# E and F loaded on 128 partitions, V and the first w_in piece in parts, a normalize one step earlier: a change to the opening of an attention and FFN kernel

## The chip, the cores and the metric

The kernel runs on one core of one Trainium2 chip. The metric is the device time of one execution in microseconds (us). The time before the change is a median of 484.24 us over three runs (483.96 to 484.36). All runs here are on one core. Some executions of a kernel can fall in a slower state (a lower granted clock, or a time over 1.5% above the fastest). None that was timed in rounds (several executions of each kernel of a call) was in it; of the single runs, whose state can't be told, only the profile is used. Times inside an execution are counted from the start of its span, as the profile counts them. PE is TensorE's matmul side, PEld its weight loads, DVE is VectorE, ACT is ScalarE, POOL is GpSimd and SP is SyncE.

## The reference

Linear attention of eight batches feeds a two-layer FFN. All inputs are float32.

```
k_proj = einsum('ks,bhsd->bhkd', E, k)      # E, F: 64 x 1024
v_proj = einsum('ks,bhsd->bhkd', F, v)      # q, k, v: 8 batches, 8 heads, 1024 tokens, 64 wide
attn   = softmax(q @ k_proj^T / sqrt(64)) @ v_proj
x      = attn, heads side by side           # 8192 x 512
h      = relu(x @ w_in)                     # w_in 512 x 2048
out    = (h * h) @ w_out                    # w_out 2048 x 512
```

## The kernel before

The kernel is one long run of matmuls: while the FFN of a batch runs, the attention of the next is slipped in between its matmuls. Only batch 0 has nothing to hide behind, so its attention is cut in half (half the tokens first). The loads of K, Q, V, w_in and w_out convert to bfloat16 on the way and go, in this order, through GpSimd's DMA queue. E and F go through SyncE's queue, as float32, on 64 partitions.

```python
    e_f32 = []
    for src in (E, F):
        t = relu_pool.tile([KP, S], F32, tag="h_relu", name="e_f32")     # 64 x 1024
        nc.sync.dma_start(t[:], src[:])
        e_f32.append(t)
    ...
    def load_heads(t, src, g):
        s = slice(4 * g, 4 * g + 4)
        nc.gpsimd.dma_start(t[:, s], rows(src, 0)[:, s])
    ...
    for g in range(2):
        load_heads(K_first, k, g)
    ident = const_pool.tile([P, P], BF16, name="ident")
    make_identity(nc, ident[:])
    load_q_half(0, slice(0, H))
    for g in range(2):
        load_heads(V_first, v, g)
    ...                                  # then w_in, the rest of Q, w_out
    def E_and_F():
        for t, src, copy in ((ET, e_f32[0], nc.vector.tensor_copy), (FT, e_f32[1], nc.scalar.copy)):
            e_bf = soft_pool.tile([KP, S], BF16, tag="expT", name="e_bf")
            copy(e_bf[:], src[:])
            ps = ffn_psum("ps_E", (P, NI, KP), BF16)
            view = e_bf[:].rearrange("k (p i) -> k i p", i=NI)
            for i in range(NI):
                nc.tensor.transpose(ps[:, i, :], view[:, i, :], ident[0:KP, 0:KP])
            copy(t[:], ps[:])
```

The stages of batch 0, in order. The fillers are matmuls whose result nobody uses; they keep PE occupied.

```python
            filler(2)
            self.project_k(0)
            filler(1)
            self.transpose_k(0)
            self.project_k(1)
            filler(2)
            self.transpose_k(1)
            filler(1)
            ...                          # transposes of Q, scores, exponentials
            self.project_v(0)
            self.copy_v(0)
            ...                          # sums, reciprocals
            self.half_values(0)
            self.half_normalize(0, 0, 0)
            self.project_v(1)
            self.copy_v(1)
            self.half_normalize(0, 0, 1)
```

The softmax here doesn't subtract the row's maximum and nothing guards it: scores larger than these inputs give would overflow.

## Time and profile before

| what | before | where it is read |
|---|---|---|
| median time | 484.24 us | the timed runs |
| span, PE busy | 482.0 us, 470.4 us | first lines of the page |
| E landed, F landed | 4.61, 5.89 us | the trace's DMA completion records |
| K's first half: the 16 DMA engines done | 7.51 to 8.25 us | same |
| first K projection starts | 8.61 us | timeline of PE |
| full clock from | 12.37 us | the trace's clock record |
| first FFN matmul | 20.01 us | timeline of PE |

The clock record gives the share of its clock that TensorE is granted. The matmuls of the K projections are 0.213 us apart ahead of the rise at 12.37 us and 0.109 after it.

The head of the page of the kernel before: PE is busy 470.4 of 482.0 us, so at most 11.6 us could be won without touching a matmul.

```profile
span 482.0 us, 8383 instructions
PE 470.4 (98%) x3614; PEld 293.1 (61%) x3614; DVE 313.2 (65%) x380; ACT 261.8 (54%) x414; POOL 33.2 (7%) x46
```

The timeline of PE from 4 to 24 us (start, duration, engine, source line, operation, output<-inputs, sizes, count; in brackets how long PE had been idle and what released it):

```profile
5.58 0.70 PE L141 MATMUL ps_E<-ident,e_bf 64*128 64x64 bf16 x8 [5.58 <-DVE e_bf L137]
7.01 0.70 PE L141 MATMUL ps_E<-ident,e_bf 64*128 64x64 bf16 x8 [0.73 <-ACT e_bf L137]
7.64 1.03 PE L360 MATMUL ps_fill<-ET 128*128 128x512 bf16 x2
8.61 1.92 PE L260 MATMUL ps_k<-K_sb,ET 128*64 128x256 bf16 x8
...
11.61 1.42 PE L260 MATMUL ps_k<-K_sb,ET 128*64 128x256 bf16 x8
...
20.01 0.81 PE L459 MATMUL ps_h<-xT,w_in 128*128 128x512 bf16 x3 [0.37 <-DVE xT L350]
```

PE transposes E, waits for F's cast, transposes F, runs two fillers and then the first K projection. The chain of work that ended last: its pieces in order of time, up to the first K projection (start, duration, what):

```profile
1.38 4.51 DMA e_f<-in_F_dram
...
5.91 1.05 ACT e_bf L137
...
7.01 0.70 PE ps_E L141 x8
7.71 0.96 PE ps_fill L360 x2
8.68 1.86 PE ps_k L260 x8
```

The chain starts with F's load and not with K's. But K is close behind: its last DMA engine finished at 8.25, less than 0.4 us before PE used it. This is the transfer view of E and F, then that of K's two halves, for the kernel before:

```profile
DMA to landing us min/median/max: 3.9/4.2/4.5
```

### The profile page before, as it was taken

Reading aid. Unit: us, or ns where it says so; the run is one execution under the profiler, and the core shown is the slowest. Engines: PE = TensorE matmul, PEld = TensorE weight load, DVE = VectorE, ACT = ScalarE, POOL = GpSimd, SP = SyncE. Lnnn points to the kernel's source line nnn. Section 1 sums busy time; section 2 is a strip of 40 time slices with the busy share of each in tenths; the row PEclk is TensorE's granted clock in tenths of the full one; section 3 lists DMA queues with packets and bytes.
Section 4 is the critical chain, followed back from the end, with each engine's and each line's share of the span. In section 5 each row is a group of like instructions: output and inputs, shape, how many; then the busy total and the mean of one; then the engine's idle time right before and its main releaser. Section 6 shows DMA issues by size and latency. Waiting matters only on the chain.

```text
span 482.0 us, 8383 instructions
## 1 busy us (share of the span) xinstructions
PE 470.4 (98%) x3614; PEld 293.1 (61%) x3614; DVE 313.2 (65%) x380; ACT 261.8 (54%) x414; POOL 33.2 (7%) x46
## 2 busy tenths in 40 slices
PE   4899999999999999999999999999999999999997
PEld 2544776475575746657475665747557474666656
DVE  1478855555958558493876748666594855948383
ACT  2488544758426664466635657176662756545351
POOL 6340020020020001000010000100000000000000
PEclk9999999999999999999999999999999999999999
DMA  9999989479989075931859147590712002020202
GB/s 162 204 204 207 170 184 203 124 128 227 172 124 238 6 176 89 192 80 64 145 87 229 13 121 131 90 196 1 173 3 81 20 1 88 1 88 0 88 0 88
DMA packets 72501, 55.46 MB, mean 115 GB/s; under 512 B 33936, under 2 KB 64656, under 8 KB 72464
## 3 DMA queue, kind: packets, MB, share of 16 engines
q0 software_dynamic: 30336, 29.36, 39.0%
q1 hardware_dynamic: 42128, 25.56, 21.2%
q8 instruction: 28, 0.46, 0.4%
q14 instruction: 9, 0.07, 0.0%
HBM read 59.24 MB, written 16.78 MB: 158 GB/s over the span
## 4 chain that ended last, share of the span: by engine, by line
PE 93%; DVE 3%; ACT 2%; DMA 1%; issue 0%; SPq 0%
PE ps_h L459 44%; PE ps_y L479 23%; PE ps_z L479 11%; PE ps_x L479 6%; PE ps_kv L178 3%; PE ps_att L219 2%; PE ps_att L204 2%; DVE hsq L518 1%; DMA e_f<-in_F_dram 1%; PE ps_k L260 1%; DVE s L473 1%; DVE xT L244 0%; ACT expT L313 0%; DVE xT L350 0%; ACT h_relu L510 0%; PE ps_fill L360 0%
## 5 line engine op out<-in xcount | busy, mean ns | idle before, releaser
L459 PE MATMUL ps_h<-xT,w_in 128*128 128x512 bf16 x1024 | 225.0, 379 | 0.4 <-DVE xT L350 0.4
L518 DVE TENSOR_TENSOR hsq<-h_relu 128x1024 bf16<-128x1024 f32 x123 | 150.0, 1223 | 76.7 <-ACT h_relu L510 76.1
L510 ACT ACTIVATE h_relu<-ps_h 128x512 f32<-128x512 f32 x256 | 149.8, 597 | 62.6 <-PE ps_h L459 62.4
L459 PEld LDWEIGHTS <-w_in 128*128 128x128 bf16 x1024 | 99.6, 98 | 117.9 <-issue 1.7
L479 PEld LDWEIGHTS <-s 128*128 128x128 bf16 x1024 | 98.5, 98 | 19.8 <-issue 8.7
L479 PEld LDWEIGHTS <-hsq 128*128 128x128 bf16 x768 | 73.8, 98 | 16.4 <-issue 2.9
L479 PE MATMUL ps_y<-T,s 128*128 128x256 bf16 x512 | 62.4, 273 | 0.0
L595 DVE TENSOR_TENSOR o_sb<-ps_z,p_b 128x512 f32<-128x512 f32 x16 | 11.1, 691 | 54.7 <-ACT p_b L591 21.1
L473 DVE TENSOR_TENSOR s<-hsq 128x1024 bf16<-128x1024 bf16 x64 | 43.5, 684 | 0.0
L591 ACT COPY o_sb<-ps_y 128x512 f32<-128x512 f32 x15 | 8.8, 586 | 54.2 <-PE ps_y L479 54.1
L211 ACT ACTIVATE expT<-ps_att 128x1024 bf16<-128x1024 f32 x28 | 27.2, 1025 | 14.0 <-PE ps_att L204 14.0
L244 DVE TENSOR_TENSOR xT<-ps_att,rs 128x1024 bf16<-128x1024 f32 x28 | 33.4, 1216 | 0.6 <-PE ps_att L219 0.6
L479 PE MATMUL ps_x<-w_out,hsq 128*128 128x256 bf16 x256 | 33.2, 273 | 0.0
L479 PE MATMUL ps_y<-w_out,hsq 128*128 128x256 bf16 x256 | 33.2, 273 | 0.0
L479 PE MATMUL ps_y<-T,hsq 128*128 128x256 bf16 x256 | 30.9, 272 | 0.0
L479 PE MATMUL ps_z<-T,s 128*128 128x256 bf16 x256 | 30.6, 273 | 0.0
L479 PE MATMUL ps_z<-w_out,s 128*128 128x256 bf16 x256 | 30.6, 273 | 0.0
L591 ACT COPY p_b<-ps_y 128x512 f32<-128x512 f32 (+1 forms) x17 | 9.4, 556 | 25.9 <-PE ps_y L479 25.8
L473 DVE TENSOR_TENSOR s<-s,hsq 128x1024 bf16<-128x1024 bf16 x32 | 21.9, 686 | 0.3
L473 DVE TENSOR_TENSOR s<-hsq,s 128x1024 bf16<-128x1024 bf16 x32 | 21.8, 684 | 0.0
L81 POOL DMA_DIRECT2D Q_sb<-in_q_dram x7 | 6.1, 877 | 226.1 <-DMA qT<-Q_sb 225.7
L591 ACT COPY p_a<-ps_y 128x512 f32<-128x512 f32 (+1 forms) x17 | 9.4, 561 | 21.8 <-PE ps_y L479 21.6
(74 smaller groups left out, 232.0 us busy)
## 6 DMA issues: line engine op xcount, KB each, us to landing
out_dram<-o_sb SPq DMA_DIRECT2D x30, 512.0 KB, 3.1
K_sb<-in_k_dram POOLq DMA_DIRECT2D x7, 1024.0 KB, 15.4
V_sb<-in_v_dram POOLq DMA_DIRECT2D x7, 1024.0 KB, 22.4
Q_sb<-in_q_dram POOLq DMA_DIRECT2D x7, 1024.0 KB, 9.8
w_in<-in_moe_w_in_dram POOLq DMA_DIRECT2D x8, 256.0 KB, 13.6
w_out<-in_moe_w_out_dram POOLq DMA_DIRECT2D x4, 512.0 KB, 13.3
K_sb<-in_k_dram POOLq DMA_DIRECT2D x2, 512.0 KB, 7.9
V_sb<-in_v_dram POOLq DMA_DIRECT2D x2, 512.0 KB, 12.7
```

The source lines that it names most:

```text
L178: nc.tensor.matmul(ps[0:KP, :], lhsT=ET[:, i, :], rhs=kv[:, :, i, :], start=f, stop=l)
L204: nc.tensor.matmul(ps[o, bank, :], lhsT=self.kT[r, 2 * pr + j, :], start=True, stop=True, rhs=self.qT[r, NT * (2 * pr + j):NT * (2 * pr + ...
L211: nc.scalar.activation(e[:], self.ps["s", pr][:], AF.Exp, scale=SCALE)
L219: nc.tensor.matmul(ps[32 * j:32 * j + 32, a, :], lhsT=weights(o, 4 * g + j), rhs=self.exp[2 * g + j // 2][o, bank, :], start=True, stop=Tr ...
L244: nc.vector.tensor_tensor(out=self.xT[:, 2 * g + e].rearrange("p a n t -> p a (n t)"), in0=self.ps["v", g, e][:], in1=self.rs[g][:], op=AL ...
L459: nc.tensor.matmul(ps[:], lhsT=w_in_blk(cb, fb), rhs=xT[:, cb, :, 2 * ch:2 * ch + 2], start=(cb == 0), stop=(cb == NCB - 1),)
L473: nc.vector.tensor_tensor(out=s[o][:, js], in0=x, in1=y, op=op)
L479: nc.tensor.matmul(ps[tb] if len(ps) == 2 else ps[0][:, tb], lhsT=lhs[:, j, tb * P:(tb + 1) * P], rhs=rhs[:, j], start=first and n == 0 an ...
L510: nc.scalar.activation(r[:, n], ps[:], AF.Relu)
L518: multiply = lambda: nc.vector.tensor_tensor(out=o, in0=r[:], in1=r[:], op=ALU.mult)
L591: nc.scalar.copy(to[:, t], ps)
L595: nc.vector.tensor_tensor(out=to[:, t], in0=ps, in1=more[:, t], op=ALU.add)
```

## The change

Its intent is to start the FFN sooner. E and F are loaded on 128 partitions (two half rows per row of E), so that the load is faster and the casts are on twice the partitions; the transposes become small matmuls that pick even or odd rows. V's second head group is loaded and projected in two parts, and all values of the first half come before the FFN. The first w_in piece is loaded in two parts. One relu goes to DVE, and in the later batches one normalize is issued one step earlier (behind step 25 instead of 26).

```diff
-        t = relu_pool.tile([KP, S], F32, tag="h_relu", name="e_f32")
-        nc.sync.dma_start(t[:], src[:])
+        t = relu_pool.tile([P, S // 2], F32, tag="h_relu", name="e_f32")
+        nc.sync.dma_start(t[:], src.rearrange("k (c s) -> (k c) s", c=2))
 ...
-    for g in range(2):
-        load_heads(V_first, v, g)
+    for s in (slice(0, 4), slice(4, 6), slice(6, 8)):
+        load_heads(V_first, v, s)
 ...
-            nc.gpsimd.dma_start(w_in_sb[j][:, g], w_in_view[:, g, :, j * fw:(j + 1) * fw])
+            for n in range(2) if (j, g) == (0, 0) else (slice(None),):
+                s = slice(n * fw // 2, (n + 1) * fw // 2) if n in (0, 1) else n
+                nc.gpsimd.dma_start(
+                    w_in_sb[j][:, g, :, s], w_in_view[:, g, :, j * fw:(j + 1) * fw][:, :, s])
 ...
+        pick = ident[:].rearrange("p (k c) -> p c k", c=2)
 ...
-            e_bf = soft_pool.tile([KP, S], BF16, tag="expT", name="e_bf")
+            e_bf = soft_pool.tile([P, S // 2], BF16, tag="expT", name="e_bf")
             copy(e_bf[:], src[:])
-            ps = ffn_psum("ps_E", (P, NI, KP), BF16)
-            view = e_bf[:].rearrange("k (p i) -> k i p", i=NI)
+            ps = ffn_psum("ps_E", (P, NI, KP))
+            view = e_bf[:].rearrange("r (p i) -> r i p", i=NI)
             for i in range(NI):
-                nc.tensor.transpose(ps[:, i, :], view[:, i, :], ident[0:KP, 0:KP])
+                for c, o in enumerate((LO, HI)):
+                    nc.tensor.matmul(ps[o, i, :], lhsT=view[:, i, :], rhs=pick[:, c, :], start=True, stop=True)
             copy(t[:], ps[:])
 ...
-            self.half_normalize(0, 0, 0)
-            self.project_v(1)
-            self.copy_v(1)
-            self.half_normalize(0, 0, 1)
+            for s in heads[1:]:
+                self.project_v(s)
+                self.copy_v(s)
+            self.half_values(1)
+            for g in range(2):
+                for e in range(2):
+                    self.half_normalize(0, g, e)
 ...
-        23: "sums 0, values 0 0, reciprocals 0", 26: "normalize 0 0",
+        23: "sums 0, values 0 0, reciprocals 0", 25: "normalize 0 0",
 ...
-                nc.scalar.activation(r[:, n], ps[:], AF.Relu)
+                if (b, ch, k, n) == (0, 0, 0, 1):
+                    nc.vector.tensor_scalar_max(r[:, n], ps[:], 0.0)
+                else:
+                    nc.scalar.activation(r[:, n], ps[:], AF.Relu)
```

Cut: the bookkeeping of the V parts, and the opening FFN steps, which no longer stop after three matmuls to wait for V's second group.

## The prediction

> **What bounds the kernel now.** The page's engine table gives PE (TensorE matmul) 470.4 us busy of a 482.0 us span; stretches of ten microseconds show PE at 10.00 of 10 almost everywhere after 40 us. PE idles 11.6 us: 5.6 at the start, about 3.5 at the end, about 2.5 between 6 and 37 us. Only the start can give anything.
>
> **What bounds the start.** The DMA stream, and behind it a chain of small steps. The timeline has the first K projection at 8.60 us, just after the first half of K landed (8.25 by the trace's DMA semaphores); later pieces land every 2.6 us per 512 KB: 10.85 (K), 13.50 (Q), 15.99, 18.54 (V), then 19.88 and 21.97 (first w_in piece; its last DMA engine lags 0.8). The first FFN matmul starts at 20.01; three run, PE waits for V's second group (projected 18.58 to 19.64, copied 19.88 to 20.29), then runs closed up from 21.10, but for 0.2 us at 24.1 while ScalarE empties the opening's four banks.
>
> **Step 1, E and F on 128 partitions.** They are issued first on 64 partitions and land at 4.61 and 5.89 us. Their 4096-byte packets take 0.16 us at first, then 0.33, and the first K packet moves only at 4.19, 2.95 us after its issue; loads issued later into an idle queue take about 1.6. The Trainium skill, "SBUF — State Buffer", section "Door 1: The DMA port swizzle", says that 64 partitions reach half of the ports; the doubled packet time agrees. On 128 partitions I expect 0.5 MB in about 1.3 us instead of some 3, so K, and the whole stream behind it, lands about 1 us earlier. The casts of E and F (0.89, 1.04 us) about halve. Added: 32 small matmuls for 16, and a float PSUM copy of ET (estimate 0.65 us, from 0.42 for 256 float columns, against 0.42); both fit before K's landing.
>
> **Step 2, V in parts.** One projection becomes two of half the columns (sum equal, or 0.3 us longer by weight loads), one copy of 0.41 us two of about 0.25. But all four normalizes (0.68 each) now queue on DVE behind both copies, and all values precede the FFN: its first matmul comes later against the chain, then runs without a break. Estimate: 0 to 0.3 us lost.
>
> **Step 3, w_in in two parts; relu on DVE.** The first part landing sooner matters little once the normalize is last. The relu on DVE should remove the 0.2 us gap. The moved later normalize lies where PE never waits: nothing.
>
> **Sum.** 1.1 us from DMA; minus 0.3, because more of K's projection runs at the cold clock (its matmuls are 0.213 us apart before 12.3 us, 0.109 after); minus 0.2 for V's order; plus 0.2 for the gap. Net 0.8 us, kept to the end because PE is saturated.
>
> **Prediction:** 483.4 us, range 482.6 to 484.3. Chances: faster by over 2% 0.01, within 2% 0.98, slower 0.01.
>
> **What would show it.** Right: E and F landed by about 4.5 us, first K packet near 3.3, K landed near 7.2, K projection near 7.4, FFN closed up from about 19.7, no gap after the opening, PE busy time within 1 us. Wrong for step 1: K still landing at 8.25, so descriptor making and not E and F held it. Wrong for step 2: the opening held by V's second copy or by DVE.
>
> **What would make it wrong.** The clock rising later (idle PE between fillers and K), a straggling DMA engine on w_in's second part, V's small matmuls bound by weight loads: then 484 or more. A stream that gains 1.5 us: 482.5.

## More of the kernel before

For later batches a table says behind which FFN step each piece of attention goes. The two entries that matter here:

```python
        23: "sums 0, values 0 0, reciprocals 0", 26: "normalize 0 0",
        28: "scores 2, scores 3, exponentials 2", 29: "exponentials 3",
```

```profile
L94 POOL DMA_DIRECT2D K_sb<-in_k_dram x2: 750/819/888, 1.2 to 2.1; - x2
DMA to landing us min/median/max: 7.0/7.9/8.7
```

K's first half was issued at 1.2 us and took 7.0 us, its second was issued at 2.1 and took 8.7.

## The result, and the profile after

The kernel after took a median of 484.84 us (six runs, 484.45 to 485.37), beside 484.3 us for the kernel before on the same chip (six runs, 483.92 to 484.5). The ratio is 1.0013, with a 95% interval from 1.0001 to 1.0026. A ratio here is the mean time of one kernel's fast runs over that of the other's from the same rounds, so it is not quite the ratio of the medians. The change was expected to save 0.8 us and cost 0.6, and the median lies above the range of 482.6 to 484.3.

One warning before the profiles are compared. The profiled execution of the kernel after took 485.37 us, the slowest of its six, and that of the kernel before took 483.81, below all six of its timed runs. The two traces therefore differ by 1.56 us, more than twice what the medians do. They show the mechanism; how much of it an average run pays must come from the timed runs.

The head of the page after: PE's busy time grew by 1.1 us and the span by 1.6.

```profile
span 483.6 us, 8454 instructions
PE 471.5 (98%) x3645; PEld 293.7 (61%) x3646; DVE 314.3 (65%) x382; ACT 260.9 (54%) x413; POOL 34.4 (7%) x48
```

The timeline of PE after, the same stretch:

```profile
4.35 2.13 PE L147 MATMUL ps_E<-ident,e_bf 128*64 128x64 bf16 x32 [4.35 <-POOL ident masks.py:199]
6.41 1.03 PE L364 MATMUL ps_fill<-ET 128*128 128x512 bf16 x2
9.78 1.86 PE L265 MATMUL ps_k<-K_sb,ET 128*64 128x256 bf16 x8 [2.33 <-DMA K_sb<-in_k_dram]
...
12.73 1.91 PE L265 MATMUL ps_k<-K_sb,ET 128*64 128x256 bf16 x8
...
22.52 1.67 PE L462 MATMUL ps_h<-xT,w_in 128*128 128x512 bf16 x7 [0.19 <-DVE xT L354]
```

E and F are transposed by 6.48 us instead of 7.71, as intended. The fillers end at about 7.44. Then PE waits 2.33 us for K, and the K projection starts 1.17 us later than before. The clock also rises later (16.04 us instead of 12.37), so the second projection takes 1.91 us where it took 1.42. PE's idle time is the likely reason. The clock record of r7 below changes in steps of 3.41 us; counted back in such steps from the two rises, PE was busy for 93% of the stretch from 8.96 to 12.37 before, and for 77% of that from 9.21 to 12.62 after. But the busy share alone does not decide it over all traces: in r5 the clock rose after a stretch with 83%, and in r1 it did not rise after one with 89%. The chain of work that ended last now begins with K:

```profile
1.25 8.49 DMA K_sb<-in_k_dram
...
9.78 1.88 PE ps_k L265 x8
```

The transfers of E and F, then of K, in the kernel after:

```profile
DMA to landing us min/median/max: 2.9/3.0/3.1
```

```profile
L93 POOL DMA_DIRECT2D K_sb<-in_k_dram x2: 747/816/886, 1.2 to 2.1; - x2
DMA to landing us min/median/max: 8.5/9.3/10.2
```

E and F land in 2.9 and 3.1 us instead of 3.9 and 4.5. K, issued at the same moment, takes 8.5 us instead of 7.0. The trace also records, for each load, when each of the 16 DMA engines was done with its share; this is where the loss becomes plain:

| load (us) | before: first, 14th, 15th, last engine | after: first, 14th, 15th, last engine |
|---|---|---|
| E | 4.00, 4.46, 4.53, 4.61 | 3.27, 3.54, 3.58, 3.65 |
| F | 5.33, 5.77, 5.82, 5.89 | 3.95, 4.19, 4.22, 4.26 |
| K, first half | 7.51, 8.04, 8.22, 8.25 | 6.68, 7.16, 8.72, 9.73 |
| K, second half | 10.27, 10.73, 10.74, 10.85 | 9.64, 10.05, 11.32, 12.32 |
| Q, first half | 12.93, 13.36, 13.36, 13.50 | 12.33, 12.69, 13.95, 14.96 |
| V, first group | 15.47, 15.89, 15.89, 15.99 | 14.85, 15.19, 16.47, 17.49 |

Fourteen engines of the kernel after finish K's first half by 7.16 us, very nearly the 7.2 that was predicted for the whole of it. Two finish at 8.72 and 9.73. The Trainium skill, "DMA: Bandwidth & Descriptors", section "Why a DMA increments its semaphore by 16 and not by 1", says that the engines of a transfer finish independently and that only the full 16 means that all data landed. The trace agrees: PE starts at 9.78, behind the last engine, with 14 of 16 shares in place for 2.6 us. GpSimd's queue shows no gap in its packets until 59.2 us, and a late engine stays late: the distance from first to last is 3.05 us for K's first half and then 2.68, 2.63, 2.64 us for the next three loads, and still 2.63 for the first w_in piece.

**Where the 1.6 us of the two traces lie.** I paired the FFN matmuls of the two kernels by number, and took the difference of their starts. The 41st FFN matmul starts at 30.63 before and at 32.68 after: +2.05 us. By the 1024th it is +1.60 (465.93 and 467.53). The +2.05 is the later K projection (+1.17) and a longer way from there to the fifth FFN matmul (12.72 us before, 13.60 after: +0.88). The 0.45 that comes back later falls mostly in five equal steps of 0.078 us, one in each of the later batches two to six; their place is the moved normalize. In the timeline of the kernel before, around 166 us, the scores of heads 2 and 3 use a PSUM bank (a piece of the memory that matmuls write to) that the normalize of line 244 still reads:

```profile
165.02 1.22 DVE L244 TENSOR_TENSOR xT<-ps_att,rs 128x1024 bf16<-128x1024 f32 x1
165.99 0.70 PE L204 MATMUL ps_att<-qT,kT 64*64 64x512 bf16 x8
166.29 0.11 PEld L204 LDWEIGHTS <-kT 64*64 64x64 bf16 x4 [0.18 <-DVE xT L244]
```

The same place after: the normalize started one step sooner and ended at 166.81, before the scores begin. There is one block of eight weight loads with no wait for DVE, and the scores take 0.63 us instead of 0.70.

```profile
165.58 1.23 DVE L249 TENSOR_TENSOR xT<-ps_att,rs 128x1024 bf16<-128x1024 f32 x1 [3.40 <-ACT rs L239]
```

```profile
167.98 0.14 PEld L209 LDWEIGHTS <-kT 64*64 64x64 bf16 x8 [0.21 <-issue]
167.98 0.63 PE L209 MATMUL ps_att<-qT,kT 64*64 64x512 bf16 x8
```

**The gap after the opening.** The relu on DVE was to close a gap of 0.2 us. The timeline of the kernel after has the two relus as follows:

```profile
25.52 2.31 ACT L516 ACTIVATE h_relu<-ps_h 128x512 f32<-128x512 f32 x4 [3.21 <-PE ps_h L462]
25.73 0.69 DVE L514 TENSOR_SCALAR h_relu<-ps_h 128x512 f32<-128x512 f32 x1 [1.48 <-PE ps_h L462]
26.17 1.82 PEld L462 LDWEIGHTS <-w_in 128*128 128x128 bf16 x9 [0.32 <-issue]
```

The next matmul starts at 26.17 us. The first relu, still on ACT, runs from 25.52 to 26.11 (0.60 us by itself); the one that moved to DVE is the second. The matmul needs the bank of the first. So the gap is what it was: 25.75 to 26.17 after, 23.70 to 24.11 before, from the start of the last matmul ahead of it to the next one; matmuls of this shape that run closed up start about 0.22 apart.

### The profile page after: what moved, and what is told of

It is laid out like the page before. It is cut to its first block, busy times and chain, and to the rows that moved or that the text cites. A ratio compares the mean times of both kernels' runs of the same rounds, so it can differ in the third digit from the quotient of the medians.

```text
span 483.6 us, 8454 instructions
## 1 busy us (share of the span) xinstructions
PE 471.5 (98%) x3645; PEld 293.7 (61%) x3646; DVE 314.3 (65%) x382; ACT 260.9 (54%) x413; POOL 34.4 (7%) x48
## 4 chain that ended last, share of the span: by engine, by line
PE 93%; DVE 3%; DMA 2%; ACT 1%; issue 0%; POOLq 0%
PE ps_h L462 44%; PE ps_y L482 23%; PE ps_z L482 11%; PE ps_x L482 6%; PE ps_kv L183 3%; PE ps_att L224 2%; DMA K_sb<-in_k_dram 2%; PE ps_att L209 2%; DVE hsq L524 1%; PE ps_k L265 1%; DVE s L476 1%; DVE xT L249 0%; ACT expT L317 0%; DVE xT L354 0%; ACT h_relu L516 0%
## 6 DMA issues: line engine op xcount, KB each, us to landing
w_out<-in_moe_w_out_dram POOLq DMA_DIRECT2D x4, 512.0 KB, 13.2
```

## The experiments

Theories when the experiments began. **T1:** E and F on 128 partitions make K late, and this alone is the loss; the rest of the change is neutral or a small gain. **T2, the rival:** the new order of V and of the opening is the loss, and K's lateness in that one profile was chance. For the cause of K's lateness three more theories were put up later and are named where they were tested. The expectations use older names: theory A is T1, M1 is T3, M2 is near to T4, and rival B (the extra loads of V and w_in make K late) falls with T2 in r4.

The calls ran on different chips: r1 to r4 on chip 9, r5 to r8 on 6, r9 to r12 on 11, r13 to r16 on 5, r17 and r18 on 10. The kernel before scattered by 0.7 us on chip 9 and by 2.0 us on chip 5, so ratios of different calls are not to be compared closely.

In the tables "K" is K's first half: the time of the first and of the last of its 16 engines. All runs from r1 to r11 and from r15 to r18 were timed in five rounds; the ratio is against the kernel before on the same chip.

### Which part of the change costs: r1 to r4 (one call)

r1 is the kernel after and r2 the kernel before, unaltered. r3 is the kernel before with only E and F taken from the change:

```diff
# r3, against before
-        t = relu_pool.tile([KP, S], F32, tag="h_relu", name="e_f32")
-        nc.sync.dma_start(t[:], src[:])
+        t = relu_pool.tile([P, S // 2], F32, tag="h_relu", name="e_f32")
+        nc.sync.dma_start(t[:], src.rearrange("k (c s) -> (k c) s", c=2))
 ...                                     # and the transposes as in the change
```

r4 is the kernel after with exactly this part taken back.

> The changed kernel once more, unaltered, for a second profile. In its first profile 14 DMA engines finished K's first half at 6.68 to 7.16 us, as predicted, but two only at 8.72 and 9.73, and the PE clock rose at 16.0 us instead of 12.4. If the two late engines are chance, K lands near 7.2 here, the clock rises near 12.5 and the span is about 481.5 to 482. If they belong to this kernel, K lands again after 8.5 and the clock rises after 14, span about 483.5. Timed ratio again 1.000 to 1.003.

> The kernel before, unaltered, for a second profile. If its start is steady: K lands at 8.2 to 8.3 us, clock rises near 12.4, ratio 0.999 to 1.001. If late DMA engines are chance in any kernel, K may land later here too and the clock rise may move by about 3.4 us.

> The kernel before with E and F on 128 partitions and nothing else. Theory A (the wide E and F loads bring the late engines and the PE idle time between fillers and K, so the clock stays low): slower than before by 0.5 to 2 us, K landing after 8.5 and clock rise after 14. Rival B (the extra descriptors of the V and w_in parts bring the late engines): K lands near 7.2 with all engines together, and the time is 0.5 to 1.0 us below before.

> The changed kernel with E and F on 64 partitions as before. Theory A: start as of before, K at 8.25, clock rise near 12.4, and 0.2 to 0.6 us below before (the later normalize gains 0.4 us by the two traces). Rival B: K lands late here too, and the time is as of the changed kernel, 0.5 us above before.

| run | median us | ratio, 95% | K | full clock from | K projection |
|---|---|---|---|---|---|
| r1, after | 484.77 | 1.0017 (1.0005 to 1.0030) | 6.68 to 9.14 | 14.66 | 9.18 |
| r2, before | 484.03 | 1.0006 (0.9993 to 1.0018) | 7.28 to 7.83 | 10.94 | 8.58 |
| r3, E and F only | 485.38 | 1.0032 (1.0018 to 1.0046) | 6.88 to 9.14 | 14.78 | 9.19 |
| r4, all but E and F | 483.61 | 0.9994 (0.9981 to 1.0006) | 7.42 to 7.88 | 12.45 | 8.55 |

T1 holds and T2 falls. E and F alone cost 0.32%, some 1.5 us; from r1 and r4 (1.0017 and 0.9994) the same part comes to 0.23%, some 1.1 us. Everything else together is no loss: 0.06% faster, with an interval that includes no change. In these four traces K's lateness repeats with E and F wide and is absent without; later traces below show it with narrow loads too. It is not always two engines: in r1 eight of the 16 were late, at 8.56 to 9.14 us. The timelines of PE, r3 first and then r4:

```profile
6.41 1.03 PE L364 MATMUL ps_fill<-ET 128*128 128x512 bf16 x2
9.19 1.86 PE L264 MATMUL ps_k<-K_sb,ET 128*64 128x256 bf16 x8 [1.74 <-DMA K_sb<-in_k_dram]
```

```profile
7.59 1.04 PE L361 MATMUL ps_fill<-ET 128*128 128x512 bf16 x2
8.55 1.92 PE L262 MATMUL ps_k<-K_sb,ET 128*64 128x256 bf16 x8
```

With E and F narrow PE goes from the fillers straight into the projection. With E and F wide it has its fillers behind it 1.2 us sooner and then waits 1.74 us.

### Descriptor making, a longer occupation of the queues, warming, and the normalize alone: r5 to r8 (one call)

Three questions about r3, and one part of the change by itself. **T3:** GpSimd makes the descriptors (the lists of moves that a load is made of) of Q's and V's loads just while K moves, and this disturbs some engines. r5 lets GpSimd read a word of K before it goes on to V, so that it makes no descriptors from 4.3 to 9.0 us. r6 loads E and F twice, to see whether holding K back for longer keeps the engines together. r7 runs six fillers instead of two, to learn what the cold clock alone costs. r8 is the kernel before with the moved normalize and nothing else.

```diff
# r5, against r3
     load_q_half(0, slice(0, H))
+    seen = const_pool.tile([P, 1], BF16, name="seen")
+    nc.gpsimd.tensor_copy(seen[:], K_first[:, 0, 0:1])
# r6, against r3
+    for n, src in enumerate((E, F)):
+        again = const_pool.tile([P, S // 2], F32, name=f"again_{n}")
+        nc.sync.dma_start(again[:], src.rearrange("k (c s) -> (k c) s", c=2))
# r7, against r3
-            filler(2)
+            filler(6)
# r8, against before
-        23: "sums 0, values 0 0, reciprocals 0", 26: "normalize 0 0",
+        23: "sums 0, values 0 0, reciprocals 0", 25: "normalize 0 0",
```

> E and F wide, else as before, and GpSimd reads a word of K's first half before it issues V's and w_in's loads, so that no descriptors are made while that half moves. Theory M1 (making descriptors slows the engines that are moving K): all 16 engines finish K's first half within 0.7 us, by 7.4, the dip of the DMA rate after 7.0 us is gone, time 0.5 to 1 us below before. Rival M2 (the queue's own cold start after an early end of E and F spreads the engines): first half still spread over 2 us and last at about 9, time as the kernel with wide E and F alone, 1.0032.

> E and F wide, else as before, and both loaded a second time into tiles nobody reads, behind the first, so that the DMA engines stay busy until about 4.8 us as with the narrow loads. M2: K's packets then start late but at full rate, the 16 engines finish its first half within 0.8 us of one another, the last at 8.0 to 8.5 us, clock rise near 12.4 or before, time within 0.3 us of before, although more bytes are moved. M1 or any other cost of the wide loads as such: last engine after 9, time 1 us or more above before.

> E and F wide, else as before, with six idle matmuls instead of two ahead of the first K projection, which end at about 9.0 us, when K lands. Clock theory: PE has no idle time of over 0.5 us before K, the clock rises near 11 to 12.4 us instead of 14.8, and of the 1.1 us that wide E and F lost at the FFN's opening 0.5 to 0.7 come back: ratio about 1.0018. Rival (only K's late landing counts): no gain, ratio 1.003.

> The kernel before with only the normalize of the later batches moved from step 26 to 25. By the two traces it saves 0.08 us in each of six batches: span 0.45 us shorter, start unchanged, ratio 0.999. Rival (the gain came from something else, such as the later DMA times): no difference in the PE times of the later batches.

| run | median us | ratio, 95% | K | full clock from |
|---|---|---|---|---|
| r5, GpSimd waits | 485.07 | 1.0015 (1.0003 to 1.0027) | 6.75 to 8.92 | 14.73 |
| r6, E and F twice | 486.53 | 1.0047 (1.0035 to 1.0059) | 8.57 to 10.62 | 17.24 |
| r7, six fillers | 485.85 | 1.0039 (1.0027 to 1.0051) | 6.74 to 9.64 | 8.96 to 12.37, then 15.79 |
| r8, normalize only | 484.32 | 1.0000 (0.9988 to 1.0012) | 7.25 to 9.51 | 13.90 |

r5: K's engines spread as before, 2.17 us from first to last, with no descriptors being made after Q's (until 3.9 us). T3 falls. r6: the second loads did not hold K back, they ran interleaved with it until 9.1 us; everything came later and the spread of 2.05 us stayed. As a test of holding it decides nothing.

r7 is the useful one. The timeline of PE:

```profile
6.41 2.71 PE L364 MATMUL ps_fill<-ET 128*128 128x512 bf16 x6
9.69 1.03 PE L264 MATMUL ps_k<-K_sb,ET 128*64 128x256 bf16 x8 [0.56 <-DMA K_sb<-in_k_dram]
...
12.56 1.91 PE L264 MATMUL ps_k<-K_sb,ET 128*64 128x256 bf16 x8 [0.79 <-DMA K_sb<-in_k_dram]
```

The first K projection ran at full clock, 1.03 us instead of 1.86. But K's second half landed at 12.52 us, PE waited for it, and the clock had fallen back to half at 12.37: the second projection took 1.91 us. Here warming PE gained nothing that could be measured (1.0039, beside 1.0032 for r3 on another chip), since the data were late. The clock record changes at 8.96, 12.37 and 15.79 us, each 3.41 us apart. The Trainium skill, "TensorE: Matmul & The Clock Gate", section "Part 1: The HAM clock gate (the "warmup" mystery)", states a free-running window of 3413 ns, and half clock after an idle window. This trace agrees with the length of the window, and the K matmuls' distances (0.213 us cold, 0.109 us warm, in the trace of the kernel before and in r7) agree with its two clocks. It does not agree with the condition: PE was busy for some 1.8 us of the window from 8.96 to 12.37, and the clock fell all the same. In r14 a window with about as much work (20.41 to 23.82) left the clock at full, so no rule follows from these traces. The time of the first rise to full clock differs by several us between traces (8.96 to 17.57 here).

r8 gives no measurable gain in time. Yet its trace has the same five steps of 0.078 us, in the same batches. So the gain of 0.39 us repeats in the trace (r4, r10 and r15 to r18, which carry the same move, have the five steps too, and no trace without it has them), and below what five rounds can tell from a ratio of 1.0000 with an interval of 0.12% on each side (0.6 us). Its profile brought something else: E and F are narrow here, and K spread by 2.27 us all the same. The last engine of F was late in that run, at 6.66 us, so an engine had fallen behind ahead of K's load.

### Is one narrow load enough, and does a third narrow one hold K: r9 to r12 (one call)

r9 is r3 with F narrow again (E stays wide); r10 is the same done to the kernel after. r11 is r3 with half of E loaded once more on 64 partitions, to occupy the engines as F did before. r12 was to let K start only when F has landed.

```diff
# r9 against r3, r10 against after
-        t = relu_pool.tile([P, S // 2], F32, tag="h_relu", name="e_f32")
-        nc.sync.dma_start(t[:], src.rearrange("k (c s) -> (k c) s", c=2))
+        if src is E:                     # as in the change
 ...
+        else:
+            t = relu_pool.tile([KP, S], F32, tag="h_relu", name="e_f32")
+            nc.sync.dma_start(t[:], src[:])
# r11, against r3
+    hold = const_pool.tile([KP, S // 2], F32, name="hold")
+    nc.sync.dma_start(hold[:], E[:, 0:S // 2])
# r12, against before
+    seen = const_pool.tile([KP, 1], F32, name="seen")
+    nc.gpsimd.tensor_copy(seen[:], e_f32[1][:, 0:1])
     for g in range(2):
         load_heads(K_first, k, g)
```

> The kernel before with E on 128 partitions and F, which is needed late, still on 64. Theory M2 (K's load spreads over the engines when they turn to it before its queue has filled; a slow load ahead of it prevents that by accident): F holds the engines until about 4.3 us, K's first half lands within 1 us over all engines, the last at 7.5 to 8.0, K projection starts at 7.6 to 8.1 instead of 8.6, 0.3 to 0.8 us below before. Rival (packets of E on 128 partitions spread K as such): spread over 2 us, last after 8.9, 0.5 to 1.5 us above before.

> The changed kernel with F alone back on 64 partitions: the candidate. M2: K as in the run of the kernel before with F narrow, plus the later normalize's 0.45 us: 0.7 to 1.2 us below before, ratio 0.9975 to 0.9985. Rival: ratio 1.0 to 1.002.

> E and F wide, else as before, with half of E loaded once more on 64 partitions behind them into a tile nobody reads, which should keep the DMA engines busy to about 4.5 us. M2: first K packets on all engines within 0.5 us of one another, spread of K's first half under 1 us, last at 7.8 to 8.4, time within 0.4 us of before though more is loaded. Rival (wide packets as such, or bytes): spread over 2 us and time as with wide E and F alone, 1.0032.

> The kernel before with narrow E and F, and K's loads issued only when F has landed, so that they meet idle DMA engines. Slower by about 3 us on purpose. M2: K's first half, landing from about 10 us on, spreads over 1.2 us or more between its first and last engine. Rival (only wide E and F spread it): spread under 0.8 us as in three of four runs with narrow E and F.

| run | median us | ratio, 95% | K | full clock from |
|---|---|---|---|---|
| r9, E wide, F narrow | 485.87 | 1.0022 (1.0010 to 1.0034) | 7.05 to 9.95 | 16.11 |
| r10, after with F narrow | 485.34 | 1.0013 (1.0001 to 1.0025) | 7.11 to 8.82 | 13.18 |
| r11, a third, narrow load | 485.47 | 1.0025 (1.0009 to 1.0042) | 6.49 to 8.75 | 12.37 |
| r12, one look | 484.32 | none | 7.26 to 8.17 | 10.20 |

Narrowing F alone does not bring K back. The third load of r11 did not hold K: K's first packet moved at 3.35 us, no later than in the kernel after (3.60), so r11 decides nothing about holding. r12 failed as an experiment: the compiler's scheduler put the wait behind K's loads, so only V's had to wait. It counts as one more trace of narrow loads.

### Does K spread because its engines start idle: r13 and r14 (one look each)

**T4:** in the wide kernels the engines are done with E and F early and begin K from idle, at different moments. r13 (narrow) and r14 (wide, on r3) fix the order of GpSimd's instructions and let it read a word of F before it issues K. Both are slower on purpose.

```diff
# r13 against before, r14 against r3
-    for g in range(2):
-        load_heads(K_first, k, g)
     ident = const_pool.tile([P, P], BF16, name="ident")
     make_identity(nc, ident[:])
+    loads = tc.manual_schedule(engines={mybir.EngineType.Pool})
+    loads.__enter__()
+    seen = const_pool.tile([KP, 1], F32, name="seen")      # [P, 1] in r14
+    nc.gpsimd.tensor_copy(seen[:], e_f32[1][:, 0:1])
+    for g in range(2):
+        load_heads(K_first, k, g)
 ...                                      # and an exit after the last load
```

> Narrow E and F, and GpSimd issues K and all later loads, in order, only when F has landed, at about 6 us; slower by 2 to 3 us on purpose. Theory M2 (a load that meets free engines spreads over them): first K packet at about 7.6, K's first half spreads over 1.2 us or more. Rival (wide packets of E and F do it): spread under 0.9 us.

> The same hold with wide E and F: K issued at about 4.3 us, first packet at about 5.9. M2: spread 1.2 us or more. If the spread came from K's packets mixing with those of E and F, it is gone here and under 0.9 us, since both have landed; r13 then tells whether it is also small with narrow loads.

The transfer view of K in r13 and then in r14:

```profile
L94 POOL DMA_DIRECT2D K_sb<-in_k_dram x2: 747/816/885, 5.8 to 6.7; - x2
DMA to landing us min/median/max: 5.6/6.4/7.3
```

```profile
L94 POOL DMA_DIRECT2D K_sb<-in_k_dram x2: 750/818/887, 4.2 to 5.0; - x2
DMA to landing us min/median/max: 5.7/6.6/7.6
```

In r13 K's engines finish between 10.88 and 11.40, in r14 between 9.32 and 9.81: 0.52 and 0.49 us apart. T4 falls (its expectation, 1.2 us or more in both, was missed), and so does "wide loads spread what follows them": in r14 the loads of E and F are wide, all engines are idle when K comes, and K stays together. A K load issued after them needs 5.6 or 5.7 us. r15 and r16, below, ran on the same chip with K issued at once, and there K's engines ended 2.60 and 1.99 us apart. In r14 the first packet moved 1.58 us after the issue. (Whole times, 487.23 and 486.85 us, are one run each and late by construction.)

### A best version, and F's transposes behind K: r15 and r16 (one call, with r13 and r14)

r15 is the kernel before with the two harmless small parts of the change, the normalize and the DVE relu. r16 is r15 with F's transposes moved behind the first K projection, since the chain before ran through F.

```diff
# r15, against before: the normalize line as in r8, and
+                if (b, ch, k, n) == (0, 0, 0, 1):
+                    nc.vector.tensor_scalar_max(r[:, n], ps[:], 0.0)
+                else:
+                    nc.scalar.activation(r[:, n], ps[:], AF.Relu)
# r16, against r15
             self.project_k(0)
-            filler(1)
+            turn(FT, F_bf, nc.scalar.copy)
             self.transpose_k(0)
```

> The kernel before with the later normalize moved and the one relu on DVE: the two small parts of the change that the traces credit, without E, F, V and w_in. The spans of the later batches shrink by 0.4 us, the gap of 0.2 us after the opening goes; ratio 0.998 to 0.9995. If the start's chance (K's spread of 0.5 to 2.3 us) outweighs that, no clear difference.

> As r15, and F's eight transposes, which only V's projection needs, moved from before the first K projection to behind it, where an idle matmul stood. In three traces with narrow loads K had landed at 7.8 to 8.25 us but its projection started at 8.55 to 8.6, behind F's cast and transposes. Theory (PE's order behind F binds there): projection at 7.9 to 8.3, 0.2 to 0.6 us below r15, ratio 0.997 to 0.999. Rival (the clock rises later because PE idles ahead of K): no gain over r15.

| run | median us | ratio, 95% | K | full clock from |
|---|---|---|---|---|
| r15 | 483.80 | 0.9983 (0.9966 to 1.0000) | 7.23 to 9.83 | 14.14 |
| r16 | 484.58 | 0.9995 (0.9980 to 1.0011) | 7.36 to 9.35 | 15.69 |

r15 is the best ratio measured, and its interval ends at 1.0000. It is not clearly faster, and it does the same work as r8 (ratio 1.0000) but for one relu that the trace shows to bring nothing. Its six runs fall in two groups: four at 483.55 to 483.82 us, two at 485.42 and 485.57. The profiled one belongs to the slow pair. In it F was late (last engine 7.62) and K spread by 2.60 us; PE waited for F's cast and transposes, and its K projection began at 10.35 us, 0.52 us behind K's last engine. I can't say whether the fast four had K together, since only one execution of a kernel leaves a trace. In r16 K itself came late, so PE waited for K and not for F; what the new order is worth stays open.

### Does it come from two queues at once: r17 and r18 (one call)

**T5:** E and F through SyncE's queue and K through GpSimd's run against each other, and this spreads K. r17 loads E and F through GpSimd's queue too, with conversion, in the order E, K's first half, F, K's second half, Q; r18 does the same on 128 partitions. Both carry r15's parts and r16's order.

```diff
# r17, against before
-        nc.sync.dma_start(t[:], src[:])
+    def load_rows(src):
+        t = soft_pool.tile([KP, S], BF16, tag="expT", name="e_bf")
+        nc.gpsimd.dma_start(t[:], src[:])
+        return t
+    E_bf = load_rows(E)
+    load_heads(K_first, k, 0)
+    F_bf = load_rows(F)
+    load_heads(K_first, k, 1)
# r18, against r17
-        t = soft_pool.tile([KP, S], BF16, tag="expT", name="e_bf")
-        nc.gpsimd.dma_start(t[:], src[:])
+        t = soft_pool.tile([P, S // 2], BF16, tag="expT", name="e_bf")
+        nc.gpsimd.dma_start(t[:], src.rearrange("k (c s) -> (k c) s", c=2))
```

> As r16, with E and F loaded on 64 partitions by GpSimd's own queue, cast to bf16 on the way: E before K's first half, F behind it. If mixing two queues spreads K: its spread is under 0.9 us and it lands at 7.3 to 8.0, K projection at 7.4 to 8.1, two casts are gone, 0.5 to 1.2 us below before, ratio 0.9975 to 0.999. If an early start as such spreads it (first packet before 4 us), spread over 1.7 us, last after 9, ratio about 1.001.

> The same on 128 partitions. Mixing theory: as r17, spread under 0.9 us, K landed at 7.3 to 8.0, ratio 0.9975 to 0.999. If wide packets of E and F as such spread K: over 1.7 us, last after 8.9, ratio 1.001 to 1.003, and r17 better by 1 us.

| run | median us | ratio, 95% | K | full clock from |
|---|---|---|---|---|
| r17, narrow | 485.20 | 1.0022 (1.0008 to 1.0035) | 7.54 to 9.32 | 17.57 |
| r18, wide | 485.27 | 1.0022 (1.0008 to 1.0035) | 7.75 to 8.95 | 15.09 |

No other queue runs at that time, and K's engines still end 1.78 and 1.20 us apart. T5 is not borne out as the sole cause. Both expectations for it were missed (a spread under 0.9 us, a ratio of 0.9975 to 0.999). The rival that r17's expectation names, an early start of K, had a spread over 1.7 us and a last engine after 9, and r17 shows 1.78 and 9.32. Both orders are slower than the kernel before. PE waits for K in r17:

```profile
9.37 1.86 PE L262 MATMUL ps_k<-K_sb,ET 128*64 128x256 bf16 x8 [2.77 <-DMA K_sb<-in_k_dram]
```

### What all traces say together

| E and F, and when K was issued | traces | K's engines apart, us |
|---|---|---|
| at least E wide, K issued at once | 9 (after, r1, r3, r5, r6, r7, r9, r10, r11) | 1.71 to 3.05 |
| narrow, K issued at once | 7 (before, r2, r4, r8, r12, r15, r16) | 0.46 to 0.91 in four, 1.99 to 2.60 in three |
| K issued only after F has landed | 2 (r13, r14) | 0.52, 0.49 |
| E and F in K's own queue | 2 (r17, r18) | 1.78, 1.20 |

Wide loads with K issued at once always left K's engines apart; narrow ones did so in some executions. In the 16 traces of the first two rows the 41st FFN matmul starts 22.2 to 23.3 us after K's last engine, though that engine's end varies from 7.83 to 10.62 us. So the FFN's start follows K's slowest engine, even if it is not in every trace K that PE waits for: with K together it was F's transposes and the fillers, and in r15 it was F.

One number sorts nearly all of these traces: when the first packet of K moved. In the 11 of the first two rows where it moved by 3.82 us, K's engines ended at least 1.71 us apart; where it moved at 4.17 us or later (the other five, r13 and r14) they ended 0.46 to 0.91 apart, and 1.99 in r16 alone. In r17 it moved at 3.90 us. This is an order found afterwards and no cause: the early packets are mostly those of the kernels with wide loads, and no run moved the first packet alone. The time for which packets of E or F and of K were in flight together does not sort them: 0.40 to 0.79 us in the four narrow traces with K together, 0.20 to 0.49 in six of the wide ones.

What makes the engines part is not settled. Descriptor making (r5), engines idle at the start (r13, r14), wide loads as such (r14) and two queues at once as the only cause (r17, r18) do not account for it. What remains possible is that K's packets and those of E and F being in flight together matters, in a way that differs from run to run; no run isolated it. The chip is an untested rival for why narrow loads differ: they kept K together in the kernel before, on chip 9 and on chip 11, and not on chips 6 and 5. Wide against narrow (chip 9), and K held against K at once (chip 5), were each compared within one chip.

## Why the prediction was wrong

**The step that failed is Step 1, "so K, and the whole stream behind it, lands about 1 us earlier".** Its first half came nearly true: E and F landed at 3.65 and 4.26 us ("by about 4.5"), K's first packet moved at 3.60 ("near 3.3"), and 14 of 16 engines had K by 7.16 ("K landed near 7.2"). It was too large even there: the packets of E and F took 2.2 us (1.76 to 3.93) where 1.3 was expected, and K's 14th engine gained 0.88 us. The term for K was -1.1 us. Measured in the trace, K came 1.48 us later (9.73 for 8.25), because the last two engines did. The prediction read a load as one event with one landing time. For one w_in load it did note a straggler, and it named "a straggling DMA engine on w_in's second part" as a danger; it did not ask the same of K, which everything waits for. r3 confirms the step by itself: E and F wide alone cost 0.32%.

It also rested on the Trainium skill, "SBUF — State Buffer", section "Door 1: The DMA port swizzle (why `[64,N]` ≈ `[32,N]`)", that 64 partitions reach half of the ports. For the two loads themselves the trace agrees: the transfers took 2.9 and 3.1 us instead of 3.9 and 4.5, and F landed 1.63 us sooner. The failure lies in carrying this gain over to the next load.

**A second weak point is the margin.** F and its transposes, not K, released PE before (chain: F's load, cast, transposes, fillers, projection). K was less than 0.4 us ahead of its use. Even a K that is earlier could only be used because F became earlier too, and a lateness of K beyond that moves the first projection by as much. The prediction said "just after the first half of K landed" and took K for the bound.

**The cold clock** was put at 0.3 us. From the K projection to the fifth FFN matmul it took 12.72 us before and 13.60 after. Over the 16 traces that issue K at once it took 12.5 to 13.0 us where the full clock came by 12.5 us (five traces), 13.2 to 13.6 where it came at 14.6 or later (seven), and 12.74 to 13.28 in the three between; r7, where it rose twice, had 13.35. So the late clock is worth some 0.5 us (an estimate from the first two ranges); the term had the right sign and was too small. The prediction did name this danger ("The clock rising later (idle PE between fillers and K)").

**Step 2, V's order, -0.2 us: in keeping with the traces.** With K on time in both, r4 against before has 12.91 for 12.72 us over that same stretch (0.19), and r1 against r3 has 13.32 for 13.24 (0.08). The split of w_in had no effect that I can find.

**"The relu on DVE should remove the 0.2 us gap": wrong, +0.2 expected and 0 measured.** The gap waits for the bank of the first relu, and the second was moved.

**"The moved later normalize lies where PE never waits: nothing": wrong by 0.39 us in the trace**, in the change's favour: five times 0.078 us of a wait by the weight loads. The prediction looked at stretches of ten microseconds, in which PE is 10.00 of 10; a wait of 0.18 us on PEld does not show there.

**The sum.** The two traces differ by +1.60 us at the end: +1.17 K, +0.88 clock and V order, -0.45 later. In an average run the loss is smaller, about 0.6 us by the medians and the ratio; as the normalize gives back 0.39, the start must lose about 1.0 on average (an estimate, from 0.6 + 0.39), where the prediction had it gain 0.8. "Within 2%" at 0.98 was right; the number and its range were not. Without its E and F part the change is 0.06% faster (r4), which can't be told from nothing.

## What to carry to other kernels

A load is complete when the slowest of its engines is, so before predicting that a load gains from room made ahead of it, look at when each engine finishes, in several executions, and ask how far the load is from being the bound. A transfer that became faster did not make the next one faster here; and in the kernel after, whose queue did not run empty, the engines that fell behind on K were still behind at the first w_in piece. Look for small gains at the waits of single instructions, on weight loads too, since busy shares over wide stretches hide them.

## What the Trainium skill lacked or had wrong

- No page that I read says how far the 16 engines of one early load can drift apart, or that the drift stays. "DMA: Bandwidth & Descriptors" says that they finish independently. Here they finished 0.46 to 3.05 us apart on K's first half, and in the kernel after the 2.6 us stayed for the loads that followed.
- The same page, section "Latency and other measured facts", has two particular engines as usually slower. The trace used here does not number the engines. In the kernel after two of 16 were late, but in r1 eight were, so this can't be the whole of it.
- The same section puts the first byte of a load through GpSimd's queue at about 1 us. In r14 the first packet of K moved 1.58 us after its issue began, with no packets of other loads in flight.
- "SBUF — State Buffer", section "Door 1", is right about the transfer: F landed at 4.26 us instead of 5.89 on 128 partitions. As advice to a kernel it lacks that the loads behind may lose more: E and F on 128 partitions alone cost 0.32% (r3).
- "TensorE: Matmul & The Clock Gate", section "Part 1", was right on the window and the two clocks: clock changes 3.41 us apart in r7, K matmuls 0.213 and 0.109 us apart. It gives half clock after an idle window; in r7 the clock fell after a window in which PE was busy for some 1.8 of 3.41 us.
